# RetNet attention and SwiGLU feed-forward on one core: the third unit's norm and the first unit's differences issued one unit earlier, and one signal from ScalarE

## The chip, the core and the metric

The kernel runs on one core of a Trainium2 chip. Five engines work side by side, each through its own queue in order: TensorE (PE; its weight loads are listed as PEld), VectorE (DVE), ScalarE (ACT), GpSimd (POOL) and SyncE (SP), which issues most of the DMAs. The metric is the device time of one execution in microseconds (us), given as the median of several runs. Before the change it is 1145.99 us, the median of 12 runs between 1143.53 and 1149.22.

## The reference

Two blocks follow each other. The first is a retention attention with 8 batches, 8 heads, 576 positions and 64 elements per head, and the second is a gated feed-forward over the 4608 resulting rows of 512.

```python
scores = scale * np.matmul(q, k.transpose(0, 1, 3, 2))
Dmat = np.where(rel >= 0, gamma[:, None, None] ** rel[None, :, :], 0.0)
attn = np.matmul(scores * Dmat[None], v)
x = attn.transpose(0, 2, 1, 3).reshape(B * S, H * D)
rms = np.sqrt(np.mean(x * x, axis=-1, keepdims=True) + 1e-06)
xn = x / rms * rms_g
g = xn @ w_gate
out = (g * (1.0 / (1.0 + np.exp(-g))) * (xn @ w_val)) @ w_out
```

Everything is float32. w_gate and w_val are 512 x 1536, w_out is 1536 x 512.

## The kernel before

**Jobs.** The attention is cut into 32 jobs, each a batch and a pair of heads. A job's positions are worked in chunks of 64. `slot(j)` (L401) puts job j's first half and job j-1's second half on the queues: `values(j-1)` (L348), products with v into two PSUM banks called `av`; `scores(j)` and `states(j)` (L276, L296), small 64x64 products; `weigh(j)` (L309) and `sums(j)` (L323) on VectorE; and `carried(j-1)` (L366), which adds the carried state into the same `av` banks and lets VectorE write the scaled result into `x` (L394). `rest=False` leaves out the half of job j-1. `following(j)` (L428) transposes q and k of job j+1 on VectorE (L255), scales its v on ScalarE (L264) and issues the loads of job j+2 on SP (L146, L210, L216).

**The tick.** `values` and `carried` use different rows of the array for the same banks. Between them stands a signal: after the last product of `values` an engine writes one number into a cell called `tick` (L363), and the first product of `carried` waits for that write (L380). Before the change the engine is GpSimd for all jobs.

**Units.** The feed-forward works in 12 units of 384 rows. Units 0 and 1 get their products plainly, `up_plain` (L599). From unit 2 on `up` (L542) uses a scheme with seven products in place of eight; its products accumulate in the banks x, y, z and w, and VectorE adds them (L561). For this the weights are combined with each other: `combine(m)` (L850) issues 12 subtractions and additions of 128x512 on GpSimd for w_val (m = 1) or w_gate (m = 0). The second product of `up` into z begins anew on what `u4` has already read from that bank.

**The out products.** `across(u)` (L661) is a generator. It makes seven products for the whole unit, in the order xo, zo, wo, yo, xo, zo, wo (n_done 0 to 6), and hands control back after each, so that the caller can put other work between them. At its start it takes two differences of blocks of h, `t1` and `b12` (L714, L715). After yo VectorE adds `u2o` and `u4o` (L685), and the second zo waits for `u4o`; the second wo waits for the difference b21 - b11 (L736). Each of four results is transposed on VectorE (L698) and stored by eight DMAs on SP (L708).

**The norm of a unit before unit 3.** `norm_0` squares x on ScalarE and sums on VectorE (L446). `norm_1` (L454) takes the mean with three products into a bank `ms`, adds epsilon on VectorE (L463) and takes the power -1/2 on GpSimd (L464). `diagonals` (L502) puts the three columns on diagonals (L506). `norm_2` (L511) spreads them with a product into a bank `rb` (L521), scales x in four operations (L523) and, from unit 2 on, takes four differences (L534) which are the operands of `up`.

**Order.** The order of the queues is that of the program text (`manual_schedule`), written out by hand in `start` (L893). The part that concerns the change is L978 to L997: unit 1's out products with the first two steps of unit 2's norm among them, then slot 8, unit 0's out products with `norm_2(2)` among them, and slot 9. `combine(1)` is issued ahead of slot 8, and `combine(0)` ahead of slot 9. Then follows `up` for unit 2. In `across(1)` the loop's index i counts products that have been issued: i = 0 is after the first.

## Time and profile before

| | |
|---|---|
| median of 12 runs | 1145.99 us |
| the profiled execution | 1145.92 us, span 1144.1 us |
| mean granted clock of TensorE | 0.994 |
| VectorE busy | 732.1 us (64%) |
| ScalarE busy | 258.8 us (23%) |
| GpSimd busy | 42.9 us (4%) |
| `across(1)`, first product to slot 8 | 188.57 to 216.63 us |
| slot 8 | from 216.63 us |
| `across(0)`, first product to slot 9 | 217.84 to 247.03 us |
| slot 9 | from 247.03 us |
| `up` of unit 2, first product | 252.63 us |

The stages' times are starts of TensorE's records in the trace. A row of the timeline gives the start and the length in us, the engine, the line, the operation, what it writes and reads, the shape and the count of merged instructions; in brackets stand the engine's idle time ahead of it and what ended it. A float32 product is recorded as two matmuls, so that the 12 products of one of `across`'s seven appear as x24. Lines named L... are those of the kernel before.

### The profile page before, as it was taken

To read this page: it belongs to the slowest core of one execution; us is meant where nothing else is said; L and a number is where in the kernel's file an instruction comes from. 1 tells how busy PE (TensorE), PEld (TensorE's weight loads), DVE (VectorE), ACT (ScalarE), POOL (GpSimd) and SP (SyncE) were. 2 spreads that over 40 slices of the span, in tenths; PEclk is the share of its full clock that TensorE was granted. 3 is DMA by queue.
4 is the path that set the end of the run, shared out by engine and by line. 5 is a ranking of instruction groups with operands and counts; after the bars stand their busy time and mean duration, and the time that the engine had idled before them with its cause. 6 is when DMAs were issued, how large, how long until landed. Compare 5 with 4: busy or idle time off the path is not lost.

```text
span 1144.1 us, 24711 instructions
## 1 busy us (share of the span) xinstructions
PE 1120.3 (98%) x10470; PEld 1047.2 (92%) x10470; DVE 732.1 (64%) x1431; ACT 258.8 (23%) x507; POOL 42.9 (4%) x65
## 2 busy tenths in 40 slices
PE   7899999989999999999999999999999999999998
PEld 6755557989999999999999999999999999999998
DVE  5788868666586586366766776466577566446352
ACT  5546642002211221211221121121121220120210
POOL 0000000470000000000000000000000000000000
PEclk8999999999999999999999999999999999999999
DMA  9764335334453566044345455305436403303304
GB/s 206 207 185 148 110 125 195 58 61 115 121 129 65 152 138 153 14 103 105 97 115 79 116 140 124 116 29 121 106 90 141 132 33 95 127 1 99 124 1 111
DMA packets 292942, 125.40 MB, mean 110 GB/s; under 512 B 270432, under 2 KB 275808, under 8 KB 292832
## 3 DMA queue, kind: packets, MB, share of 16 engines
q1 hardware_dynamic: 282688, 107.66, 38.1%
q10 hardware_dynamic: 10144, 16.16, 4.4%
q8 instruction: 82, 1.34, 0.5%
q14 instruction: 28, 0.23, 0.1%
HBM read 108.83 MB, written 14.94 MB: 108 GB/s over the span
## 4 chain that ended last, share of the span: by engine, by line
PE 93%; DVE 2%; POOL 2%; DMA 1%; issue 1%; ACT 1%; SPq 0%; DVEq 0%; POOLq 0%; ACTq 0%
PE x L554 14%; PE w L554 14%; PE z L554 13%; PE up L611 10%; PE xo L676 8%; PE wo L676 8%; PE zo L676 8%; PE y L554 7%; PE yo L676 4%; PE av L355 2%; PE av L374 1%; POOL w_gate L858 1%; PE s L284 1%; PE s L304 1%; DVE sum L333 1%
## 5 line engine op out<-in xcount | busy, mean ns | idle before, releaser
L578 ACT COPY m<-x 128x384 f32<-128x384 f32 x60 | 28.7, 478 | 355.0 <-PE x L554 355.0
L676 PE MATMUL xo<-h,w_out 128*128 128x192 f32 x528 | 90.3, 328 | 0.0
L554 PE MATMUL x<-x,w_gate 128*128 128x192 f32 x480 | 89.3, 329 | 0.0
L554 PE MATMUL w<-sums,w_val 128*128 128x192 f32 x480 | 88.6, 328 | 0.3
L554 PE MATMUL x<-x,w_val 128*128 128x192 f32 x480 | 88.8, 328 | 0.0
L554 PE MATMUL z<-x,w_val 128*128 128x192 f32 x480 | 87.8, 326 | 0.0
L554 PE MATMUL z<-x,w_gate 128*128 128x192 f32 x480 | 87.8, 326 | 0.0
L554 PE MATMUL w<-sums,w_gate 128*128 128x192 f32 x480 | 87.8, 326 | 0.0
L676 PEld LDWEIGHTS xo<-h,w_out 128*128 128x128 f32 x528 | 85.9, 190 | 0.6
L676 PE MATMUL wo<-h,w_out 128*128 128x192 f32 x504 | 85.3, 326 | 0.0
L561 DVE TENSOR_TENSOR u<-m,y 128x384 f32<-128x384 f32 x60 | 33.1, 552 | 79.1 <-PE y L554 79.1
L676 PEld LDWEIGHTS wo<-h,w_out 128*128 128x128 f32 x504 | 82.5, 190 | 0.0
L554 PEld LDWEIGHTS w<-sums,w_val 128*128 128x128 f32 x480 | 79.2, 190 | 2.7 <-DVE c L561 2.7
L554 PEld LDWEIGHTS x<-x,w_gate 128*128 128x128 f32 x480 | 79.8, 191 | 0.5
L554 PEld LDWEIGHTS x<-x,w_val 128*128 128x128 f32 x480 | 79.2, 190 | 0.6
L554 PEld LDWEIGHTS z<-x,w_val 128*128 128x128 f32 x480 | 79.7, 190 | 0.0
L554 PEld LDWEIGHTS z<-x,w_gate 128*128 128x128 f32 x480 | 79.7, 190 | 0.0
L554 PEld LDWEIGHTS w<-sums,w_gate 128*128 128x128 f32 x480 | 79.5, 190 | 0.0
L561 DVE TENSOR_TENSOR h<-u,w 128x384 f32<-128x384 f32 x60 | 33.0, 551 | 70.9 <-PE w L554 70.9
L573 ACT ACTIVATE h<-h 128x384 f32<-128x384 f32 x90 | 47.0, 523 | 88.6 <-DVE h L561 88.6
L611 PE MATMUL up<-x,w_gate 128*128 128x384 f32 x192 | 63.3, 488 | 0.9 <-DVE x L523 0.7
L611 PE MATMUL up<-x,w_val 128*128 128x384 f32 x192 | 62.7, 487 | 0.0
(184 smaller groups left out, 1778.7 us busy)
## 6 DMA issues: line engine op xcount, KB each, us to landing
w_out<-w_blocks SPq DMA_DIRECT2D x70, 768.0 KB, 4.9
out_dram<-o SPq DMA_DIRECT2D x368, 24.0 KB, 1.6
qraw<-in_q_dram SPq DMA_DIRECT2D x96, 72.0 KB, 2.6
kraw<-in_k_dram SPq DMA_DIRECT2D x96, 72.0 KB, 2.7
k<-in_k_dram SPq DMA_DIRECT2D x48, 128.0 KB, 3.0
v<-in_v_dram SPq DMA_DIRECT2D x48, 128.0 KB, 2.9
w_out<-in_moe_w_gate_dram ACTq DMA_DIRECT2D x5, 1024.0 KB, 5.6
w_out<-in_moe_w_out_dram ACTq DMA_DIRECT2D x3, 1024.0 KB, 4.8
```

The source lines that it names most:

```text
L284: nc.tensor.matmul(s[side(odd), e, i * L : i * L + L], lhsT=d["kT"][side(e), c * L : c * L + L], rhs=d["qT"][side(e), c * L : c * L + L], ...
L304: nc.tensor.matmul(o[side(e)], lhsT=d["k"][side(odd), i, e], rhs=d["v"][side(odd), i, e], start=True, stop=True,)
L333: nc.vector.scalar_tensor_tensor(out=t[:, c], in0=t[:, c - 1], scalar=gc[:, hp : hp + 1], in1=part, op0=ALU.mult, op1=ALU.add,)
L355: mm = nc.tensor.matmul(av[odd][column(j, odd, e), i * L : i * L + L], lhsT=d["v"][side(odd), i, e] if c < NC - 1 else d["vt"][:, e], rhs= ...
L374: mm = nc.tensor.matmul(av[odd][column(j, odd, e), i * L : i * L + L], lhsT=d["sum"][side(e), c - 1], rhs=d["qT"][side(e), c * L : c * L + L],
L554: nc.tensor.matmul(ps[:, i * HU : i * HU + HU], lhsT=w_up[m][:, 2 * blk + c, cut], rhs=t_of[u][blk][:, c], start=(start and i == c == 0), ...
L561: nc.vector.tensor_tensor(out=o, in0=a, in1=pairs_of(ps), op=ALU.add)
L573: nc.scalar.activation(out=o, in_=c, func=AF.Silu)
L578: nc.scalar.copy(out=s1, in_=pairs_of(x_))
L611: nc.tensor.matmul(ps[:, :U], lhsT=w_up[m][:, 4 * half + c, i * P : i * P + P], rhs=x_of[u][:, c], start=(c == 0), stop=(c == NHP - 1),)
L676: nc.tensor.matmul(ps[:, i * HU : i * HU + HU], lhsT=a[:, c, i * P : i * P + P], rhs=rhs[:, c], start=(start and i == c == 0), stop=False, ...
L858: nc.gpsimd.tensor_tensor(out=o, in0=a, in1=b, op=op)
```

## The change

There are four edits. The two differences at the head of `across` become a function `differences(u)` of its own, which `across` calls unless they were made already. In unit 1's out products unit 0's differences are issued after the second product, behind `norm_0(2)`. `norm_1(2)` and `diagonals(2)` move from after the fourth product to after the third, and `norm_2(2)` moves from unit 0's out products (after the third) into unit 1's (after the fifth). For job 8 alone, `values` writes the tick with a ScalarE copy in place of GpSimd's memset.

```diff
-        d["valued"] = nc.gpsimd.memset(tick, 0.0)
+        if j == 2 * NHP:
+            d["valued"] = nc.scalar.copy(out=tick, in_=mhalf[:1])
+        else:
+            d["valued"] = nc.gpsimd.memset(tick, 0.0)
         follow(d["valued"], mm)
...
+    t1_of = {}
+
+    def differences(u):
+
+        h = h_of[u]
+        b11, b12, b22 = h[:, :NH, :HU], h[:, :NH, HU:], h[:, NH:, HU:]
+        t1 = t1_of[u] = ffn.tile([P, NH, HU], F32, tag="t1", name=f"t1_{u}")
+        for o, a, b in ((t1, b12, b11), (b12, b22, b12)):
+            nc.vector.tensor_tensor(out=o, in0=a, in1=b, op=ALU.subtract)
+
     def across(u):
...
-        t1 = ffn.tile([P, NH, HU], F32, tag="t1", name=f"t1_{u}")
...
-        block(t1, b12, b11, ALU.subtract)
-        block(b12, b22, b12, ALU.subtract)
+        if u not in t1_of:
+            differences(u)
         yield
...
-        product(t1, z, True)
+        product(t1_of.pop(u), z, True)
...
         for i, _ in enumerate(rest):
             if i == 1:
                 norm_0(2)
-            elif i == 3:
+                differences(0)
+            elif i == 2:
                 norm_1(2)
                 diagonals(2)
+            elif i == 4:
+                norm_2(2)
         rest = across(0)
         next(rest)
         combine(1)
         slot(8, rest=False)
         following(8)
-        for i, _ in enumerate(rest):
-            if i == 2:
-                norm_2(2)
+        for _ in rest:
+            pass
         combine(0)
         slot(9)
         following(9)
```

## The prediction

> **What bounds the kernel now.** I read the page first: one engine fills the span.

> ```profile
> span 1144.1 us, 24711 instructions
> PE 1120.3 (98%) x10470; PEld 1047.2 (92%) x10470; DVE 732.1 (64%) x1431; ACT 258.8 (23%) x507; POOL 42.9 (4%) x65
> ```

> TensorE (PE) is busy for 98%, so 1144.1 - 1120.3 = 23.8 us are idle, and some busy time may be at a lower clock. A change to other engines' work can only win where PE waits or runs slowly. So second, PE's waits:

> ```profile
> PE av L374 <- POOL tick L363: 3.7, 3, 3.1
> PE zo L676 <- DVE u4o L685: 0.8, 1, 0.8
> ```

> Columns: total us, times, longest. One wait of 3.1 us for GpSimd's (POOL's) tick, one of 0.8 us for VectorE's (DVE's) `u4o`. Third, PE in order of time, for where these lie; slot 10 stands beside slot 9 as the same work undisturbed:

> ```profile
> 239.04 4.17 PE L676 MATMUL zo<-h,w_out 128*128 128x192 f32 x24 [0.78 <-DVE u4o L685]
> 247.03 0.69 PE L355 MATMUL av<-ret,v 64*64 64x64 f32 x32
> ...
> 252.01 0.69 PE L374 MATMUL av<-qT,sum 64*64 64x64 f32 x32 [3.13 <-POOL tick L363]
> 252.63 2.35 PE L554 MATMUL x<-x,w_gate 128*128 128x192 f32 x8
> ...
> 257.02 1.46 PE L554 MATMUL z<-x,w_gate 128*128 128x192 f32 x8
> ...
> 272.71 0.69 PE L355 MATMUL av<-ret,v 64*64 64x64 f32 x32
> ...
> 277.66 1.46 PE L554 MATMUL z<-x,w_gate 128*128 128x192 f32 x8
> ```

> Both waits are in or just behind `across(0)`. From the first `av` to product z slot 9 takes 257.02 - 247.03 = 9.99 us, slot 10 takes 4.95. Fourth, POOL, and PE by stretches (length, busy, granted clock, DMA share, GB/s):

> ```profile
> 215.16 19.27 POOL L858 TENSOR_TENSOR w_val<-w_val 128x512 f32<-128x512 f32 x12 [7.41 <-PE wo L676]
> 234.39 17.54 POOL L858 TENSOR_TENSOR w_gate<-w_gate 128x512 f32<-128x512 f32 x12
> 251.87 0.09 POOL L363 MEMSET tick<- 1x1 f32 x1
> ```

> ```profile
> 252.00:257.00 5.00, 4.99 (x48) 0.66 0.26 43
> ```

> The tick, 0.09 us of work, is queued behind both combines (36.7 us without a break); in shorter stretches the clock is at 0.50 from about 253.2 to 256.7. Last, DVE:

> ```profile
> 236.42 1.51 DVE L534 TENSOR_TENSOR sums<-x,sums 128x384 f32<-128x384 f32 x1
> 237.85 0.54 DVE L685 TENSOR_TENSOR u2o<-m1o,yo 128x384 f32<-128x384 f32 x1
> 238.43 0.55 DVE L685 TENSOR_TENSOR u4o<-u2o,zo 128x384 f32<-128x384 f32 x1
> ...
> 257.05 0.77 DVE L255 STREAM_TRANSPOSE qT<-qraw 128x576 f32<-128x576 f32 x1
> 257.74 0.74 DVE L255 STREAM_TRANSPOSE kT<-kraw 128x576 f32<-128x576 f32 x1
> 258.40 0.13 DVE L1018 TENSOR_SCALAR rms_k<-rms_g 128x4 f32<-128x4 f32 x1
> ...
> 259.09 0.55 DVE L561 TENSOR_TENSOR u<-u,z 128x384 f32<-128x384 f32 x1
> ...
> 280.33 0.55 DVE L561 TENSOR_TENSOR u<-u,z 128x384 f32<-128x384 f32 x1
> ```

> `yo` was done at 234.4, but its reader began at 237.85, behind `norm_2(2)`.

> **The change part by part.**

> *Job 8's tick on ScalarE (ACT).* Job 8's last L355 product ends at 247.84. ACT is idle from 236.6 to 255.0 before, so its copy can run at about 248. No such copy is in the trace; the nearest row, ACT's 1x1 activation at L904, took 0.203 us, POOL's memset 0.09. Cost 0.11 us more, from below 0 (both are hidden), at most 0.11: in slot 10 the tick is done 0.6 us before PE reaches L374. I take 0 because the scores and states (L284, L304) cover it. ACT holds at the tick from 222.6 (after the `m1o` copy) to 248. Queued behind it: job 10's four scalings, which ran at 234.8 to 236.6 and will run at about 248 to 250 (needed in slot 10, near 267), and the `m` copy of the first up product, whose x is ready near 250 and whose reader comes after 254. No cost; past 4 us of delay the `m` copy would hold DVE. SP and POOL queues lose nothing else.

> PE then runs slot 9 as it runs slot 10: 9.99 - 4.95 = 5.04 us gained. Of that about 3.3 is the wait and 1.7 the clock. [...] The row shows the half clock 1.2 us after this gap, and full clock in slots 10 to 12, which have the same small products and no gap. I take the row, 5.04, and keep 3.3 for the range.

> *The next wait in slot 9.* With the tick gone DVE is late next. In slot 10 `u4` (L561, `u<-u,z`) ends 280.33 + 0.55 - 272.71 = 8.17 us after the slot's start, and PE's second product into z begins at 8.85 (281.56), 0.68 later. In slot 9 two transposes for job 10 and `rms_k` stand ahead of the two adds: 258.44 - 257.05 = 1.39 us. `u4` ends at 8.17 + 1.39 = 9.56, PE goes 0.06 later (as at 238.98 to 239.04): 9.62 - 8.85 = 0.77 us lost, at most 0.9 with the slower restart. Before, the tick's wait hid this. If the records are loose by the slack, it is 0: bounds 0 to 0.9, I take 0.77.

> *`norm_2(2)` leaves `across(0)`.* From yo to the last wo, 230.29 to 243.04, is 12.75 us; the same three products in the next unit take 341.82 - 330.12 = 11.70. Gain 1.05 us (0.78 waiting, the rest a slow restart). DVE then adds `u2o` at 234.4 and `u4o` by 235.6, and zo can go at 238.1.

> *What moves into `across(1)`.* On PE: the six ms records (0.56 us, one product earlier) and the two rb records (0.65 us, from `across(0)`): 0 in sum. On DVE: `differences(0)`, two of 1.35 us (the L688 rows without POOL beside them; 2.3 with), after the gathers that end at 198.04; t1's reader zo ended at 196.5, so about 198.0 to 200.7. This lies in DVE's idle 6.33 us before 204.37. Then r, POOL's power (0.85 to 1.77), the diagonals: done near 203 to 204. The one step PE waits for in this unit, the subtraction b21 - b11, is issued ahead of `norm_2` and ends near 210.8, for a product at 213.3. `norm_2`'s eight operations follow, 2.19 + 4 x 0.57 = 4.5 us, to about 215.2; its product rb waits for diagonals that are 5 us old. Behind them the result (0,1) comes 2.4 us later (213 to 215.4), and its eight stores with it. No moved step issues a DMA itself. SP's 32 stores took 18.8 us, so they may push job 10's loads (226.6) by 2.4 us; these land some 7 us later and are needed near 253. Without that slack each us would cost PE one.
> One thing the trace does not show: which PSUM bank rb gets. One that is long free costs 0; that of x would make PE wait for the transpose of `xo`, from 208.7 to 209.6, 0.9 us. Less than 0 is excluded: PE is full there. I take 0: no wait of PE in this stage names a transpose (L698).

> *POOL.* `combine(1)` starts 0.65 us later. Without the moved DVE work beside it (2.34 against 1.35 us for DVE, and POOL's operations 1.27 to 2.39) both combines may end near 250. Nothing on PE needs that end: the first weights, group 0, are written by about 240. Cost and gain 0; the later groups are used at 268 and 289.

> **Sum.** -5.04 + 0.77 - 1.05 = -5.3 us. The profiled execution took 1145.92 us (span 1144.1), the median is 1145.99, so the same subtraction holds: 1140.7 us, span about 1138.8.

> **Rivals.**
> *Loss given back* (0.14): rb waits for the bank (0.9), or slot 9 has a pause for "issue" as slot 11 had (1.10 us), so far hidden in the tick's wait. 1140.7 + 1.0 = 1141.7. For it: three such pauses are on PE's list, 3.4 us in all; against: of the 25 slots from 8 on, one shows it.
> *POOL still holds PE* (0.05): if the first `w_gate` product waited for the whole of `combine(0)`, it would start near 251.9 in place of 252.63 and keep the low clock: 0.7 gained, 1145.3. Against: POOL began `w_val` at 215.16, while wo still read other rows of that tile until 216.7, so waits are by region.
> *Slower* (0.03): the DVE work moved into `across(1)` delays b21 - b11 and so the last product. Place: L688 near 210. It has 2.5 us of slack, after an idle stretch of 6.3 us into which about 4.5 us go. It decides only when the moved work outgrows both and the gain: 6.3 + 2.5 + 5.3 = 14 us ahead of that step, against 4.5. With 17 us the time is 1149. Only POOL's company stretched such rows (1.7 times), and POOL is idle there.

> **How the numbers follow.** The forecast has 0.78. A measurement here tells 0.2% (2.3 us) from no change. Faster by more: forecast, given-back loss: 0.92. Within: 0.05, slower 0.03. Low end: no `u4` wait and slot 11's pause gone, 5.3 + 0.8 + 1.1 = 7.2: 1138.8. High end: 3.3 for the tick in place of 5.04 (1142.4), with some of the given-back loss: 1143.0.

> **What would show it.** Right: L374 in slot 9 without a wait; clock 1.0 throughout 240 to 260; zo in `across(0)` without a wait for `u4o`; a new wait of about 0.8 us of z at L554 for DVE `u`, near 255; rb at about 208.7. Wrong: a wait on rb, on wo of `across(1)`, or of the first up product for POOL; or a half clock in slot 9 without a gap.

## The result and the profile after

The changed kernel takes 1141.24 us (median of 12 runs, 1138.71 to 1143.58) against 1145.75 us for the kernel before (48 runs, those shown earlier among them). The ratio is 0.9958, 95% interval 0.9948 to 0.9969: 4.5 us less. The profiled execution took 1142.27 us with a span of 1140.4.

TensorE's waits, as total, times and longest in us. In the kernel after, the lines from L366 on are numbered higher (L374 is L377, L554 is L557, L561 is L564, L676 is L688). "issue" stands for time in which the engine waited for nothing that the profile shows:

```profile
PE av L377 <- issue: 3.4, 4, 2.1
...
PE av L377 <- POOL tick L366: 0.8, 3, 0.3
...
PE z L557 <- DVE u L564: 0.7, 1, 0.7
```

The wait of 3.1 us for the tick and the one for `u4o` are gone; a wait of z for `u` is new. Of the four waits for "issue", the two below 0.5 us lie in slots 10 and 11, the others at the start of the kernel. TensorE in order of time:

```profile
190.10 4.06 PE L688 MATMUL xo<-w_val,w_out 128*128 128x192 f32 x24
...
231.82 4.06 PE L688 MATMUL yo<-h,w_gate 128*128 128x192 f32 x24
235.72 4.06 PE L688 MATMUL xo<-h,w_out 128*128 128x192 f32 x24
239.62 4.06 PE L688 MATMUL zo<-h,w_out 128*128 128x192 f32 x24
243.52 4.06 PE L688 MATMUL wo<-h,w_out 128*128 128x192 f32 x24
247.52 0.69 PE L355 MATMUL av<-ret,v 64*64 64x64 f32 x32
...
252.47 1.46 PE L557 MATMUL z<-x,w_gate 128*128 128x192 f32 x8
...
257.23 1.54 PE L557 MATMUL z<-x,w_gate 128*128 128x192 f32 x8 [0.70 <-DVE u L564]
...
271.63 0.35 PE L377 MATMUL av<-qT,sum 64*64 64x64 f32 x9 [0.34 <-issue]
```

From yo to the last wo of `across(0)` there are now 11.70 us in place of 12.75. Slot 9 reaches its z product after 252.47 - 247.52 = 4.95 us in place of 9.99. The second z waits 0.70 us. The clock (length, busy, granted clock, DMA share, GB/s) of the stretch where it was 0.66, and of 240 to 260 us, for which the prediction asked for 1.0:

```profile
252.00:257.00 5.00, 4.53 (x28) 1.00 0.28 46
240.00:260.00 20.00, 19.30 (x244) 1.00 0.33 55
```

The profile's span falls by 3.7 us, and the stage that was changed by more. From the first xo of `across(1)` to the first xo of `across(2)` it is 317.68 - 188.57 = 129.11 us before and 314.00 - 190.10 = 123.90 after: 5.21 less. The start of the kernel, which the change doesn't touch, was 1.53 us longer in this execution, and everything behind the stage is equal to 0.02 us. So all comparisons of profiles below take the stage, counted from that first xo.

### The profile page after: what moved, and what is told of

Same layout as the page of the kernel before. It is cut to its first block, busy times and chain, and to the rows that moved or that the text cites. A ratio compares the mean times of both kernels' runs of the same rounds, so it can differ in the third digit from the quotient of the medians.

```text
span 1140.4 us, 24713 instructions
## 1 busy us (share of the span) xinstructions
PE 1120.8 (98%) x10470; PEld 1047.7 (92%) x10470; DVE 726.7 (64%) x1431; ACT 258.8 (23%) x508; POOL 39.7 (3%) x64
## 4 chain that ended last, share of the span: by engine, by line
PE 96%; DVE 1%; DMA 1%; ACT 1%; issue 1%; SPq 0%; DVEq 0%; POOL 0%; POOLq 0%; ACTq 0%
PE x L557 14%; PE w L557 14%; PE z L557 14%; PE up L614 10%; PE xo L688 8%; PE wo L688 8%; PE zo L688 8%; PE y L557 7%; PE yo L688 4%; PE av L355 2%; PE av L377 2%; PE s L284 2%; PE s L304 1%; PE turn_q L234 1%; PE ms L475 1%
## 5 line engine op out<-in xcount | busy, mean ns | idle before, releaser
L688 PE MATMUL xo<-h,w_out 128*128 128x192 f32 x528 | 90.3, 328 | 0.0
L557 PE MATMUL w<-sums,w_val 128*128 128x192 f32 x480 | 88.6, 328 | 0.3
L557 PE MATMUL x<-x,w_val 128*128 128x192 f32 x480 | 88.7, 328 | 0.0
L557 PE MATMUL z<-x,w_gate 128*128 128x192 f32 x480 | 87.9, 326 | 0.7 <-DVE u L564 0.7
L557 PE MATMUL x<-x,w_gate 128*128 128x192 f32 x480 | 88.5, 328 | 0.0
L557 PE MATMUL z<-x,w_val 128*128 128x192 f32 x480 | 87.8, 326 | 0.0
L557 PE MATMUL w<-sums,w_gate 128*128 128x192 f32 x480 | 87.8, 326 | 0.0
L688 PEld LDWEIGHTS xo<-h,w_out 128*128 128x128 f32 x528 | 85.9, 190 | 0.6
L688 PE MATMUL wo<-h,w_out 128*128 128x192 f32 x504 | 85.3, 326 | 0.0
L564 DVE TENSOR_TENSOR u<-m,y 128x384 f32<-128x384 f32 x60 | 33.1, 552 | 79.1 <-PE y L557 79.1
L688 PEld LDWEIGHTS wo<-h,w_out 128*128 128x128 f32 x504 | 82.5, 190 | 0.0
L557 PEld LDWEIGHTS w<-sums,w_val 128*128 128x128 f32 x480 | 79.2, 190 | 2.7 <-DVE c L564 2.7
L557 PEld LDWEIGHTS z<-x,w_gate 128*128 128x128 f32 x480 | 79.6, 190 | 1.0 <-issue 1.0
L557 PEld LDWEIGHTS x<-x,w_val 128*128 128x128 f32 x480 | 79.2, 190 | 0.6
L557 PEld LDWEIGHTS x<-x,w_gate 128*128 128x128 f32 x480 | 79.3, 190 | 0.5
L557 PEld LDWEIGHTS z<-x,w_val 128*128 128x128 f32 x480 | 79.7, 190 | 0.0
L557 PEld LDWEIGHTS w<-sums,w_gate 128*128 128x128 f32 x480 | 79.5, 190 | 0.0
L564 DVE TENSOR_TENSOR h<-u,w 128x384 f32<-128x384 f32 x60 | 33.0, 550 | 69.5 <-PE w L557 69.4
```

The source lines that it names most:

```text
L557: nc.tensor.matmul(ps[:, i * HU : i * HU + HU], lhsT=w_up[m][:, 2 * blk + c, cut], rhs=t_of[u][blk][:, c], start=(start and i == c == 0), ...
L564: nc.vector.tensor_tensor(out=o, in0=a, in1=pairs_of(ps), op=ALU.add)
L688: nc.tensor.matmul(ps[:, i * HU : i * HU + HU], lhsT=a[:, c, i * P : i * P + P], rhs=rhs[:, c], start=(start and i == c == 0), stop=False, ...
```

## The experiments

**The tick alone, and the moves alone.** The first kernel is the one before with job 8's tick on ScalarE; the second is the changed one with that tick left on GpSimd. They tell how the gain is shared.

```diff
-        d["valued"] = nc.gpsimd.memset(tick, 0.0)
+        if j == 2 * NHP:
+            d["valued"] = nc.scalar.copy(out=tick, in_=mhalf[:1])
+        else:
+            d["valued"] = nc.gpsimd.memset(tick, 0.0)
```

> The kernel before with job 8's tick written by ScalarE; norm and differences stay where they were. Theory (two separate waits): slot 9 runs like slot 10, its second z product is 4.95 us after the first av product in place of 9.99, the clock stays at 1.0, then the wait for u4 of about 0.9 us appears; the 0.78 us wait of zo in across(0) stays. Gain 5.04 - 0.9 = 4.1 us, about 1141.6 us. Rival (the gain comes from GpSimd and VectorE being relieved): under 2 us, above 1143.7.

Measured: 1144.87 us against 1145.67, ratio 0.9996 (0.9985 to 1.0008), which can't be told from no change. By the number the rival holds. By the profile both fall. Slot 9 does what the theory says (the first w_val product of unit 2 comes 70.87 us into the stage, against 74.95 before: 4.08 earlier), and most of the gain is lost one slot later, at a place that neither names:

```profile
257.47 1.54 PE L557 MATMUL z<-x,w_gate 128*128 128x192 f32 x8 [0.70 <-DVE u L564]
...
273.80 0.58 PE L377 MATMUL av<-qT,sum 64*64 64x64 f32 x9 [2.26 <-issue]
274.31 2.92 PE L557 MATMUL x<-x,w_gate 128*128 128x192 f32 x8
```

In slot 10, among the small products of `carried`, TensorE stands for 2.26 us with nothing that it waits for in the profile ("issue"), and runs at half clock behind it (x takes 2.92 us in place of 1.57):

```profile
273.80:277.00 3.20, 3.20 (x17) 0.50 0.02 5
```

At the first xo of `across(2)` the stage is 127.82 us, only 1.29 below the kernel before.

For the moves alone the edit puts the single memset back into the changed kernel.

> The changed kernel with job 8's tick left on GpSimd. Theory: the wait of zo goes (1.05 us); GpSimd's combines end near 251, about 0.9 us earlier, and TensorE comes to the tick 1.0 us earlier, so the wait for the tick stays at about 2 to 3 us. If the gap alone (about 2 us) does not halve the clock, the gain is 1.05 + 5.04 - 2 = 4.1 us (1141.6), with the wait for u4 hidden; if the clock falls as after the gap of 3.13 us, 2.4 us (1143.3). Rival (parts add up: the moves are worth only their own wait): gain 1.05, 1144.7.

Measured: 1143.13 us, ratio 0.9978 (0.9967 to 0.9988), a gain of 2.5. TensorE first, then its clock, then GpSimd:

```profile
248.56 0.69 PE L374 MATMUL av<-qT,sum 64*64 64x64 f32 x32 [1.69 <-POOL tick L363]
```

```profile
252.00:257.00 5.00, 4.70 (x29) 1.00 0.40 66
```

```profile
214.84 16.84 POOL L867 TENSOR_TENSOR w_val<-w_val 128x512 f32<-128x512 f32 x12 [13.62 <-PE wo L685]
231.64 16.83 POOL L867 TENSOR_TENSOR w_gate<-w_gate 128x512 f32<-128x512 f32 x12
```

The two combines take 33.6 us without the moved VectorE work beside them, against 36.7 before. In the stage they end 2.5 us earlier, where the theory had 0.9, and TensorE comes 1.0 us earlier. So the wait for the tick shrinks from 3.13 to 1.69 us, below the 2 to 3 that the theory had, and the clock stays full; a wait of z for `u` of 0.30 us is left. The stage is 125.47 us, 3.64 shorter. The moves shorten the wait for the tick as well as removing their own; the additive rival (1.05 us) falls. The median's gain of 2.5 (1.4 to 3.8 by the interval) is smaller than the stage's; the profiled execution, at 1141.34 us, was the third fastest of 20, and what the others lost is not shown.

By the medians the parts give 0.8 and 2.5 us alone, and 4.9 together on the same chip (the next run); with intervals of 1 us and more to each side, these don't tell whether the parts add up. The stages of the profiles give 1.29 and 3.64, and 5.21 and 4.48 for the two profiles of the changed kernel. What needs a cause is the tick alone: it wins 4.08 us in slot 9 and keeps 1.29.

> The changed kernel unaltered, beside the others on one chip: about 4.5 us below the kernel before; in the profile, the stage from the first xo of across(1) to the first w_val product of unit 2 should be 5.2 us shorter than before, whatever the start of the kernel does.

Measured: 1140.74 us, ratio 0.9958 (0.9941 to 0.9974). Up to the first w_val product the stage is 69.80 us, 5.15 shorter than before and the same to 0.01 us as in the first profile of this kernel; slots 10 and 11 have pauses of 0.52 and 1.02, where the first profile had 0.34 and 0.47, and so the whole stage, to the first xo of `across(2)`, is 124.63 us, 4.48 shorter than before.

**What makes the pause.** In the kernel with the tick alone, SP shows what goes out ahead of it:

```profile
240.94 17.89 SPq L711 DMA_DIRECT2D out_dram<-o  x32
258.93 2.01 SPq L146 DMA_DIRECT2D qraw<-in_q_dram  x4
...
266.07 1.07 SPq L659 DMA_DIRECT2D w_out<-w_blocks  x2
```

SP is busy in one piece: 32 stores of unit 0's results, job 11's loads, then two block loads of 768 KB each. Slot 10 begins at 269.34, 3.3 us behind these. In the kernel before slot 10 came 7.6 us behind them, since the tick's wait held TensorE back but not SP. In the changed kernel unit 0's stores begin 9.15 us ahead of slot 9 in place of 6.82, because `norm_2` no longer stands in front of the first result on VectorE, and so the block loads go out earlier too. The test gives the kernel with the tick alone a longer lead by another way: it issues the two block loads ahead of job 11's loads (only the lines on SP's order):

```diff
         slot(9)
-        following(9)
+        prepare_next(9)
+        fetch()
+        fetch()
+        load_next(9)
...
-                if i in (1, 3):
+                if i == 3 or i == 1 and u > 2:
```

> The tick alone on ScalarE, with unit 2's first two block loads (w_out from w_blocks, 768 KB each) issued on SP ahead of job 11's loads instead of behind them, some 7 us earlier. Theory (TensorE's pause for "issue" in slot 10 is its instructions' transfer waiting behind these loads): the pause of 2.26 us and the half clock after it (1.7 us) go; slot 12 starts 4 to 5 us earlier after across(1)'s start than in the kernel before, in place of 1.3; the median falls from 1144.9 to about 1141.3. Rival (the pause belongs to the place in TensorE's stream or to the new timing as such, whatever is on the queues): the pause stays and the median is above 1144.

Measured: 1142.26 us against 1146.45, ratio 0.9965 (0.9947 to 0.9984). The block loads go out at 260.67, and slot 10, from 271.21, runs without a pause and at full clock:

```profile
272.84 0.68 PE L377 MATMUL av<-qT,sum 64*64 64x64 f32 x31
273.46 1.57 PE L557 MATMUL x<-x,w_gate 128*128 128x192 f32 x8
```

The stage is 125.18 us, 3.93 below before in place of 1.29. The median is 1 us above the 1141.3 of the theory, but the kernel before was slower beside it too (1146.45 against 1145.67): the gain is 4.2 us, where 4.4 was expected. In slot 11, where the next pair of loads, left in its place, comes 4.7 us ahead, there is a pause of 1.24 us, as there was one of 1.10 before.

The trace also has a transfer whose end fits the pause. The page lists queues of kind "instruction" (packets, MB, share of the 16 DMA engines):

```profile
q8 instruction: 82, 1.34, 0.5%
```

By an estimate from the counts its packets are TensorE's: 82 packets of 16 KB for 20940 matmuls and weight loads are one for 255, and in the kernel before they go with these records rather than with the time: 2 from 75 to 195 us, beside 783 records, 5 from 253 to 303, beside 1081, and 8 from 977 to 1124, beside 1808. In the kernel with the tick alone one of them falls into slot 10. It starts at 271.46 and ends at 272.41; the pause is from 271.54 to 273.80. DMA from 271.40 to 271.50:

```profile
q1 hardware_dynamic: 6, 0.02, 62.9%
q8 instruction: 1, 0.02, 59.1%
```

All profiles together, for slot 10; the third column is the end of that packet, counted from the start of the slot:

| kernel | block loads ahead of slot 10, us | instruction packet ends, us | pause, us |
|---|---|---|---|
| tick alone | 3.27 | 3.07 | 2.26 |
| late transposes | 4.72 | 1.63 | 0.80 |
| differences back | 5.44 | 0.99 | 0.34 |
| after | 5.47 | 1.07 | 0.34 |
| after, again | 5.93 | 1.21 | 0.52 |
| moves alone | 6.67 | 0.59 | 0 |
| before | 7.59 | 0.21 | 0 |
| tick, early loads | 10.54 | 0.22 | 0 |
| late transposes, early loads | 11.71 | 0.91 | 0.30 |
| after, early loads | 13.19 | 0.81 | 0 |

The pause goes with the packet in these ten profiles: there is none where it ended 0.85 us or less into the slot, and one where it ended at 0.91 or later. Slot 11 is alike (in nine of these kernels the packet ends 1.55 to 2.16 us into it, with pauses of 0.47 to 1.24; with the tick alone at 0.85, without a pause). All 15 pauses of the two slots end 1.2 to 1.6 us after the packet, and those of slot 10 stand before the same nine products. By this timing TensorE waits for its own instructions; no view names what ends the pause. That moving the loads ends slot 10's pause is shown by this run; that the packet is late because the loads use the same 16 DMA engines is read from the timing. The lead of the loads alone doesn't decide, as the next to last row shows: there job 11's loads stand between.

**The new wait of z.** The changed kernel with job 10's transposes, its scalings and `rms_k` behind the first two adds:

```diff
-        following(9)
+        load_next(9)
...
         start()
-        nc.vector.tensor_scalar(
-            out=rms_k, in0=rms_g, scalar1=3.0 / 8.0 * K1, scalar2=None, op0=ALU.mult
-        )
+        turns.append(9)
```

(The scalings belong to `prepare_next(9)`; `rms_k` is then computed behind it.)

> The changed kernel with job 10's two transposes and rms_k put behind the first two VectorE adds of unit 2's first up product, as in the later slots. Theory: they alone caused the new wait of z for u4 (0.70 us, 0.93 with the restart), which goes; slot 9 becomes like slot 10; about 0.9 us below the changed kernel, near 1140.3. Rival (something else in slot 9 is late by then, such as the copy m or the banks): no more than 0.3 us.

Measured: 1140.94 us, ratio 0.9959 (0.9945 to 0.9972), no difference from the changed kernel's 1140.74 beside it. The cause is confirmed, the gain is not:

```profile
253.65 1.46 PE L557 MATMUL w<-sums,w_gate 128*128 128x192 f32 x8
254.95 1.46 PE L557 MATMUL z<-x,w_gate 128*128 128x192 f32 x8
```

z follows w at once, and the first w_val product comes 68.89 us into the stage, 0.91 earlier. But TensorE then reaches slot 10 only 4.72 us behind the block loads and pauses for 0.80 in place of 0.34 to 0.52, and the stage ends at 123.74, between 0.2 and 0.9 below the two profiles of the changed kernel.

So both repairs were tried, the early loads on the changed kernel and on this one.

> The changed kernel with the same two block loads issued earlier. Theory: its pause of 0.34 to 0.52 us in slot 10 goes, the wait of z for u4 stays at 0.70 us; some 0.4 us below the changed kernel, if job 11's loads, about 1 us later, delay nobody. Rival: no difference, or a later wait of slot 11 for its loads.

Measured: 1140.55 us, ratio 0.9958 (0.9936 to 0.9979). The pause in slot 10 is gone, slot 11 has one of 0.80; the stage is 123.91, that of the first profile of the changed kernel. The expected 0.4 us does not show in the stage, and the times can't tell it.

> Both repairs: job 10's transposes behind the first adds, and the two block loads earlier. Theory: neither the wait of z for u4 (0.93 us with the restart) nor slot 10's pause (0.80 us in the kernel with the late transposes); 1.3 us below the changed kernel, about 1139.6. Rival (the two waits cover each other, so that only the larger counts): 0.9 us.

Measured: 1140.41 us against 1146.45, ratio 0.9945 (0.9923 to 0.9967). The wait of z is gone; a pause of 0.30 stays in slot 10, though the blocks lead by 11.7 us (job 11's loads now stand between), and one of 1.02 in slot 11. The stage is 123.51, the shortest of all. Its ratio is the lowest, but the interval overlaps that of the changed kernel, and the stage is 0.39 us below one profile of that kernel, whose two profiles differ by 0.73. The expected 1.3 us below the changed kernel is not shown.

**Where the differences lie.** The changed kernel without `differences(0)` in `across(1)`.

> The changed kernel with unit 0's differences back at the head of across(0). Theory: they lie in VectorE's free time in either place; TensorE's stage from the first xo of across(1) to the first w_val product of unit 2 is the same within 0.1 us, and VectorE's two rows grow from 1.35 to about 2.3 us beside GpSimd. Rival (GpSimd relieved of them matters): the stage is longer by over 0.5 us.

One execution was measured: to the first w_val product the stage is 69.80 us, equal to the changed kernel. On VectorE:

```profile
220.74 1.32 DVE L672 TENSOR_TENSOR t<-h 128x1152 f32<-128x1152 f32 x1
222.09 2.31 DVE L672 TENSOR_TENSOR h<-h 128x1152 f32<-128x1152 f32 x1
```

Only one of the two rows grew; TensorE doesn't notice, and in the changed kernel this part is worth nothing by itself. GpSimd notices it:

```profile
218.07 19.00 POOL L870 TENSOR_TENSOR w_val<-w_val 128x512 f32<-128x512 f32 x12 [13.62 <-PE wo L688]
237.02 17.06 POOL L870 TENSOR_TENSOR w_gate<-w_gate 128x512 f32<-128x512 f32 x12
```

The two combines take 36.0 us here, against 33.7 in the changed kernel. So most of the 3.1 us by which the moves free GpSimd comes from these two differences. They would matter where GpSimd still writes job 8's tick; no run has that.

**How long a gap halves the clock.** The prediction's sum had 1.7 us for the half clock behind a gap of 3.13 us, from one row, and the high end of its range, with 3.3 us for the tick, had none. Two kernels, one execution each, put a gap into every slot from 10 on: copies of an otherwise unused 128x160 tile on ScalarE (5 to 14, by job) stand between the last product of `values` and the tick.

```diff
-            d["valued"] = nc.gpsimd.memset(tick, 0.0)
+        for i in range(n):
+            one = nc.scalar.copy(out=idle, in_=idle)
+            if i == 0:
+                follow(one, mm)
+        d["valued"] = nc.scalar.copy(out=tick, in_=idle[:1, :1])
```

> The changed kernel with the tick of jobs 9 to 31 delayed on purpose by 5 to 14 idle ScalarE copies, so that TensorE stands still in every slot from 10 on, for about 1.2 to 4.1 us in steps. [...]

> As the kernel with rising gaps, with other lengths in another order (13, 8, 11, 6, 10, 9, 12 copies), to part the length of the gap from the place of the slot. If the length decides, the half clock follows the copies in both; if the phase of a free-running window decides, equal lengths near the bound differ from slot to slot.

They took 1229.84 and 1241.2 us. 46 gaps that end on the tick, with what followed each in the next 7 us:

| gap, us | gaps | followed by half clock |
|---|---|---|
| 1.02 to 1.79 | 10 | 0 |
| 2.09 to 2.50 | 6 | 1 |
| 2.71 to 3.22 | 15 | 11 |
| 3.42 to 4.49 | 15 | 15 |

Two slots of the first kernel with the same gap went different ways. The second view has the 6 us behind each (length, busy, granted clock, DMA share, GB/s):

```profile
616.74 1.13 PE L388 MATMUL av<-qT,sum 64*64 64x64 f32 x32 [2.86 <-ACT tick L378]
...
894.09 0.69 PE L388 MATMUL av<-qT,sum 64*64 64x64 f32 x32 [2.86 <-ACT tick L378]
```

```profile
616.74:622.74 6.00, 6.00 (x47) 0.50 0.01 3
894.09:900.09 6.00, 6.00 (x65) 1.00 0.00 0
```

Equal gaps go both ways, so it isn't the length alone. In each of the two executions the half-clock stretches start and end on one grid of 3.413 us: the 39 starts and ends that can be read from rows of 0.5 us behind the gaps lie within 0.01 us of it. Divided by this grid, the first of the two gaps of 2.86 us leaves TensorE standing for 2.16 us within one period, the second for 1.28 and 1.58 us in two. Over all 46 gaps the half clock followed where TensorE stood for 2.00 us or more within one period (27 gaps), and not where it was 1.81 us or less (19 gaps). By length, no gap of up to 1.79 us was followed by the half clock, all of 3.42 us and more were, and 12 of the 21 between. The half clock cost 1.5 to 3.1 us each time, by an estimate: half of the 3.0 to 6.2 us for which it lasted behind the restart. In the kernel before, the period that ends at 253.26 us, where the half clock begins, holds 2.16 us of the gap; with the tick alone, the one that ends at 273.73 us holds 2.19 us of the pause.

## Why the prediction was right

It said 1140.7 us from 1138.8 to 1143.0; the median is 1141.24. Its terms, against the profile after:

- **The tick**, 5.04: slot 9 takes 4.95 us to z, as slot 10 did. 5.04. The 1.7 for the clock are in it: from x to z are 257.02 - 252.63 = 4.39 us before and 252.47 - 249.76 = 2.71 after.
- **The next wait**, 0.77 lost, at most 0.9: the wait is 0.70, and the product after it begins 258.60 - 247.52 = 11.08 us into the slot, against 10.15 in slot 10 of before. 0.93 lost, just above the bound. The late transposes show the cause.
- **`norm_2` out of `across(0)`**, 1.05: 12.75 - 11.70 = 1.05.
- **What moves into `across(1)`**, 0: xo there to slot 8 is 28.06 us before and 28.71 after, the 0.65 of rb. rb ran at 210.27 behind xo, without a wait for a bank; that rival is out, and so is the one that GpSimd still holds PE.
- **Sum**, -5.3: -5.04 + 0.93 - 1.05 = -5.16, and -5.15 is measured up to the first w_val product.

The mechanism and the sizes held. Two things in the working didn't.

First, it treated the tick and the moves as separate items and said of the tick that SP loses nothing. By that a tick alone would have given 4.3 us; its profile gives 1.29, and its times no change that can be told. When TensorE comes 4 us earlier and SP doesn't, slot 10 comes 3.27 us behind the block loads in place of 7.59, and the instruction packet ends 3.07 us into it in place of 0.21. That this cost so little in the changed kernel was luck: the moves also let unit 0's stores start 2.3 us earlier ahead of slot 9, and the prediction counted these stores only in `across(1)`, as a delay. So the clearing of `across(0)` is worth its 1.05 us plus most of what the tick alone loses in slot 10.

Second, the pause for "issue" was expected as a risk in slot 9. It came in slots 10 and 11 (0.34 and 0.47 in the first profile, 0.52 and 1.02 in the second, against 0 and 1.10 before), so it hardly changed the sum.

The median fell by 4.5 us where the stage of the first profile fell by 5.2. Three things may be in the difference. In the second profile of the changed kernel the stage fell by 4.48, with longer pauses. The start differed by up to 3.7 us between the profiles (first xo of `across(1)` from 187.49 to 191.14 us). And by the figures of the gap runs a gap of 3.13 us, divided by the grid at random, stays below 1.81 us in both parts in one execution of seven, and below 2.00 us in one of four, so that a typical execution of the kernel before loses 0.2 to 0.4 us less than the profiled one, an estimate. How much each counts is not shown; there is one profile of the kernel before.

## What to carry to other kernels

A small signal that is queued behind long work on a slow engine can hold the busiest engine: here a write of 0.09 us, behind 36.7 us of GpSimd's work, held TensorE for 3.13 us. Moving it to an engine that was idle at that time took this wait away. But an engine that is let go early runs ahead of the queues that were not: with the tick alone TensorE won 4.08 us and lost most of it to a pause of 2.26 us one slot later. Before counting a gain, follow SP's queue too and ask which transfers the earlier work now meets, the instruction packets among them. And count a gap of TensorE of 2.1 to 3.2 us at its length plus a chance of the half clock behind it, which followed 12 of 21 such gaps here.
